# A fixed order on four engines, weights converted in small steps, and reciprocals on transposed sums

## The chip, the cores and the metric

The kernel runs on one core of a Trainium2 chip. TensorE (PE in the profile, with its weight loads as PEld) multiplies matrices, VectorE (DVE) and ScalarE (ACT) work element by element out of SBUF and PSUM, GpSimd (POOL) does so out of SBUF, and SyncE (SP) issues DMAs here. The engines run their own queues of instructions and wait for each other through semaphores. The metric is the device time of one execution in microseconds, the median of several; lower is better.

## The reference: what is computed

Attention over 4 batches and 8 heads with 768 positions and 64 dimensions, in which a query sees only the keys whose six hash bits are the same as its own; then a feed-forward layer over the 3072 rows of 512.

```python
q_bits = np.einsum('bhsd,dk->bhsk', q, proj) > 0        # 6 bits; k_bits likewise
mask = q_bucket[:, :, :, None] == k_bucket[:, :, None, :]
scores = np.where(mask, q @ k.T / np.sqrt(64), -1e9)
attn = np.exp(scores - scores.max(-1)); attn = attn / (attn.sum(-1) + 1e-9)
x = (attn @ v)                                          # as (3072, 512)
h = x @ w_in                                            # w_in (512, 2048), double precision
out = (h * (1 / (1 + np.exp(-1.702 * h)))) @ w_out      # w_out (2048, 512), double precision
```

q, k, v and proj come in single precision, the two weight matrices as 64-bit floats, which the kernel turns into 32-bit ones itself.

## The kernel before

**Pairs and units.** `attention` walks over 16 pairs: one batch and two heads, which lie on the two halves of the 128 partitions. A pair has two halves of 384 queries (`c` = 0, 1), and each half six blocks of 128 keys (`kt`). One (`c`, `kt`) is a unit; a pair has twelve. A unit is two bf16 matmuls on hash bits and two 32-bit ones on kT and qT into the score tile `ps` (L210, two buffers in PSUM), an exp on ACT from `ps` into the tile `e` (L211), a running sum `acc` of the exps on DVE (`sums`, L220 to L230, with POOL adding blocks 2 and 3 into `two`, L224), and the matmuls with v into `av` (L237). `values` runs two units behind `scores` (`LAG`). After the last unit of a half, `norm` sums `acc` over the partitions on PE (`dn`, L245), inverts all 128×384 sums (L247), and writes the quotient to `xT` (L249, L251).

**Preparing the next pair.** `steps_of(n + 1)` gives nine steps, one per unit of pair n: first `measure`, which on ACT squares k and q and keeps the largest sums (a guard read at the very end, L200); then for k and for q two groups of three PE transposes (`tp`, L155), copied to kT by DVE (L158) and to qT by ACT (L160), and two hash matmuls (L165), whose bits DVE writes (L166, L168). `tp`, `hash` and `dn` share two PSUM slots (tag `m`). k and q have one SBUF buffer each, so a load of the next k waits until both the transposes and `measure` are through with the last one. SP issues these loads.

**Weights.** `convert` turns a chunk of 128×512 doubles into floats: POOL issues its DMA (L104), DVE does six operations (L110 to L115 and L120), POOL a square (`size`, L118) and an addition (L119). There are 16 chunks of w_in and 16 of w_out. The text calls `convert` twice per pair.

**Order.** Only PE has its order written out (`manual_schedule(engines={PE})`); what stands on DVE, ACT, POOL and SP, and in which order, a scheduler decides by its own estimates.

**Feed-forward.** `feed_forward` takes six blocks of 512 rows: sixteen hidden tiles `h` (four matmuls each, L384, four PSUM buffers) with a gelu on ACT into `g` (L386), then four output tiles `y` (sixteen matmuls each, L390), copied by DVE (L393) and stored by SP. A second attention and a second feed-forward stand in an `If` that is taken only where `measure` found large values; it is not taken here.

Of the kernel before, what the change touches and what calls it, by code (L numbers as in the profile page):

```python
# [16 lines left out]
PE = mybir.EngineType.PE  # L17

P = 128
# [14 lines left out]
def kernel(  # L34
# [67 lines left out]
    def convert(cv, dst, src):  # L102
        raw = cv.tile([P, CW, 2], U32, tag="raw", name="raw", bufs=2)
        nc.gpsimd.dma_start(out=raw, in_=src)  # L104
        lo, hi = raw[:, :, 0], raw[:, :, 1]
        sign = cv.tile([P, CW], U32, tag="sign", name="sign")
        bits = cv.tile([P, CW], U32, tag="bits", name="bits")
        size = cv.tile([P, CW], F32, tag="size", name="size")

        nc.vector.tensor_scalar(sign, hi, 0x80000000, 0x40000000, op0=Alu.bitwise_and, op1=Alu.bitwise_or)  # L110
        nc.vector.tensor_scalar(bits, hi, 3, 0x7FFFFFFF, op0=Alu.logical_shift_left, op1=Alu.bitwise_and)  # L111
        nc.vector.tensor_tensor(bits, bits, sign, op=Alu.bitwise_xor)  # L112

        nc.vector.tensor_scalar(sign, bits, 0xFF800000, None, op0=Alu.bitwise_and)  # L114
        nc.vector.scalar_tensor_tensor(dst, lo, 2.0**-52, sign.bitcast(F32), op0=Alu.mult, op1=Alu.mult)  # L115


        nc.gpsimd.tensor_tensor(size, hi.bitcast(F32), hi.bitcast(F32), op=Alu.mult)  # L118
        nc.gpsimd.tensor_tensor(dst, bits.bitcast(F32), dst, op=Alu.add)  # L119
        nc.vector.scalar_tensor_tensor(dst, size, (1.125 * 2.0**-15) ** 2, dst, op0=Alu.is_ge, op1=Alu.mult)  # L120
# [3 lines left out]
    chunks = [(w_in_sb[:, kc, f : f + CW], wi[kc, :, f : f + CW]) for f in range(0, FF, CW) for kc in range(KC)]  # L124
    chunks += [(w_out_sb[:, fc, d : d + CW], wo[fc, :, d : d + CW]) for fc in range(FC) for d in range(0, DM, CW)]
# [13 lines left out]
    def prepare(wk, mps, tiles, scale, out_of):  # L139
# [5 lines left out]
        for name, off, op in (("k", k_off, Alu.is_gt), ("q", q_off, q_op)):  # L145
# [5 lines left out]
            def turned(c, name=name, x=x, xt=xt):  # L151
                cols = slice(c * HS, (c + 1) * HS)
                tp = mps.tile([P, HT, P], F32, tag="m", name="tp")
                for i in range(HT):
                    nc.tensor.transpose(tp[:, i, :], x[:, c * HT + i].rearrange("p j d -> p (j d)"), ident)  # L155
                tp = tp.rearrange("p t s -> p (t s)")
                if name == "k":
                    nc.vector.tensor_copy(xt[:, cols], tp)  # L158
                else:
                    nc.scalar.mul(xt[:, cols], tp, scale)  # L160
# [13 lines left out]
    def attention():  # L174
        actx = ExitStack()
        with actx:
            cv = actx.enter_context(tc.tile_pool(name="cv", bufs=1))
# [37 lines left out]
            def sums(n, c, kt):  # L215
                e = es[c]
                if kt == 1:
                    acc = st.tile([P, 2, HS], F32, tag="acc", name="acc")
                    accs[n, c] = acc
                    nc.vector.scalar_tensor_tensor(acc, e[:, 0, :, 0:HS], T * TINY, e[:, 1, :, 0:HS],  # L220
                                                   op0=Alu.add, op1=Alu.add)
                elif kt == 3:
                    two = st.tile([P, 2, HS], F32, tag="two", name="two", bufs=1)
                    nc.gpsimd.tensor_tensor(two, e[:, 2, :, 0:HS], e[:, 3, :, 0:HS], op=Alu.add)  # L224
                    accs[n, c, 2] = two
                elif kt > 3:
                    acc = accs[n, c]
                    nc.vector.tensor_tensor(acc, acc, e[:, kt, :, 0:HS], op=Alu.add)  # L228
                    if kt == T - 1:
                        nc.vector.tensor_tensor(acc, acc, accs.pop((n, c, 2)), op=Alu.add)  # L230
# [8 lines left out]

            def norm(n, c):  # L240
                b, hp = pairs[n]
                acc, av = accs.pop((n, c)), avs.pop((n, c))
                dn = mps.tile([P, HS], F32, tag="m", name="dn")
                for j in range(2):
                    nc.tensor.matmul(dn[D * j : D * (j + 1), :], ones, acc[:, j, :], start=True, stop=True)  # L245
                rd = st.tile([P, HS], F32, tag="rd", name="rd")
                nc.vector.reciprocal(rd, dn)  # L247
# [6 lines left out]
            def steps_of(n):  # L254
                ready[n] = {}
                return [lambda: measure(n)] + prepare(wk, mps, tiles[n], 1.0 / D**0.5, ready[n])

            with tc.manual_schedule(engines={PE}):
                fetch(0)
                for f in steps_of(0):  # L260
                    f()
                per = -(-len(chunks) // len(pairs))
                behind = []
                LAG = 2
                for n in range(len(pairs)):
                    todo = []
                    if n + 1 < len(pairs):
                        fetch(n + 1)
                        todo = steps_of(n + 1)
                    convs = chunks[n * per : (n + 1) * per]  # L270
                    for u in range(2 * T):
                        c, kt = divmod(u, T)
                        scores(n, c, kt)
                        behind.append((n, c, kt))
                        sums(n, c, kt)
                        if len(behind) > LAG:
                            x = behind.pop(0)
                            values(*x)
                            if x[2] == T - 1:
                                norm(x[0], x[1])  # L280
                        if u >= 1 and todo:
                            todo.pop(0)()
                        if u % 6 == 2 and convs:
                            convert(cv, *convs.pop(0))
                    for f in todo:
                        f()
                    for x in convs:
                        convert(cv, *x)
                for x in behind:
                    values(*x)  # L290
                    if x[2] == T - 1:
                        norm(x[0], x[1])

                nc.vector.tensor_reduce(largest, sizes, axis=AX.X, op=Alu.max)
                row = mps.tile([1, P], F32, tag="m", name="row")
                nc.tensor.transpose(row, largest, ident)
                nc.vector.tensor_reduce(largest[0:1, 0:1], row, axis=AX.X, op=Alu.max)
# [73 lines left out]
    def feed_forward(tag):  # L371
        NT = 512
        G = NT // P
        outv = out.rearrange("(b p t) d -> b t p d", b=B, p=P)
        with ExitStack() as fctx:
            gp = fctx.enter_context(tc.tile_pool(name=f"gp{tag}", bufs=2))
            op = fctx.enter_context(tc.tile_pool(name=f"op{tag}", bufs=4))
            fps = fctx.enter_context(tc.tile_pool(name=f"fps{tag}", bufs=4, space=PSUM))
            for n in range(N // NT):
                g = gp.tile([P, FC, NT], F32, tag="g", name="g")  # L380
                for fc in range(FC):
# [4 lines left out]
                    nc.scalar.activation(g[:, fc, :], h, Act.Gelu_apprx_sigmoid)  # L386
                for i in range(G):
# [9 lines left out]
    attention()  # L397
    feed_forward("")
# [32 lines left out]
```

## Time and profile before

| | us |
|---|---|
| median of 3 runs (1212.72 to 1213.97) | 1213.66 |
| the profiled execution | 1212.9 |
| its span, first to last instruction | 1211.1 |
| PE busy, share of the span | 1125.0, 93% |
| DVE busy | 437.9, 36% |
| ACT busy | 257.9, 21% |
| POOL busy | 160.6, 13% |
| mean granted clock of PE | 0.967 |

In the rows of the profile, `L247 DVE RECIPROCAL rd<-dn` names the line, the engine, the operation and the tile written and read; a group of equal instructions has its count, busy us, mean ns of one, and the idle time of the engine ahead of them with what ended it. Timeline rows begin with the start and the duration in us. A 32-bit matmul is two records, so that a hidden tile of four matmuls counts as eight. The busy shares are means over stages that differ, so the prediction reads them stage by stage.

### The profile page before, as it was taken

How to read it: one execution, taken by the hardware profiler on the slowest of the kernel's cores; microseconds unless marked ns; L12 is line 12 of the kernel's file. 1: busy time of each engine (PE TensorE's matmuls, PEld its weight loads, DVE VectorE, ACT ScalarE, POOL GpSimd, SP SyncE). 2: the span in 40 equal slices, each digit the busy share in tenths (PEclk: the TensorE clock that was granted, in tenths of full speed). 3: DMA queues.
4: the chain of work that ended last, by engine and by line, in shares of the span. 5: the costliest groups of instructions: out<-in, count | busy, mean ns of one | idle time of the engine just before them, and what ended most of it. 6: DMA issues, size and time to landing. Idle time of an engine off the chain costs nothing.

```text
span 1211.1 us, 9543 instructions
## 1 busy us (share of the span) xinstructions
PE 1125.0 (93%) x3905; PEld 456.5 (38%) x3905; DVE 437.9 (36%) x582; ACT 257.9 (21%) x386; POOL 160.6 (13%) x136
## 2 busy tenths in 40 slices
PE   5858677689999999989999999999999999999997
PEld 2222222233333333324444444444444444444443
DVE  6989899986666666660000000000000000000000
ACT  3322322234444444432100100110011001001100
POOL 4545454531111111110000000000000000000000
PEclk9788988889999999999999999999999999999999
DMA  7233223311212112000000000000000000000000
GB/s 171 75 94 109 80 94 96 96 44 40 53 42 50 40 40 53 14 2 0 1 17 18 0 9 17 9 1 9 27 0 1 17 18 0 9 17 9 1 18 19
DMA packets 83539, 42.64 MB, mean 35 GB/s; under 512 B 76320, under 2 KB 76320, under 8 KB 83488
## 3 DMA queue, kind: packets, MB, share of 16 engines
q1 hardware_dynamic: 78880, 25.18, 8.4%
q0 software_dynamic: 4608, 16.78, 3.9%
q8 instruction: 32, 0.52, 0.2%
q14 instruction: 19, 0.16, 0.0%
HBM read 35.65 MB, written 6.29 MB: 35 GB/s over the span
## 4 chain that ended last, share of the span: by engine, by line
PE 78%; DVE 18%; POOL 3%; issue 1%; DMA 1%; ACT 0%; DVEq 0%; POOLq 0%
PE h L384 27%; PE y L390 27%; PE ps L210 9%; PE av L237 8%; PE hash L165 3%; DVE bits L112 2%; DVE rd L247 2%; DVE acc L228 2%; DVE bits L111 2%; PE tp L155 1%; POOL w_in_sb L119 1%; PE dn L245 1%; POOL w_out_sb L119 1%; DVE sign L114 1%; DVE sign L110 1%
## 5 line engine op out<-in xcount | busy, mean ns | idle before, releaser
L384 PE MATMUL h<-xT,w_in_sb 128*128 128x512 f32 x768 | 332.3, 595 | 3.2 <-DVE xT L251 3.2
L390 PE MATMUL y<-w_out_sb,g 128*128 128x512 f32 x768 | 330.6, 592 | 0.0
L393 DVE COPY o<-y 128x512 f32<-128x512 f32 x24 | 16.6, 691 | 645.4 <-PE y L390 645.4
L384 PEld LDWEIGHTS h<-xT,w_in_sb 128*128 128x128 f32 x768 | 146.4, 191 | 187.7 <-issue 187.7
L390 PEld LDWEIGHTS y<-w_out_sb,g 128*128 128x128 f32 x768 | 145.9, 190 | 183.7 <-issue 183.7
L211 ACT ACTIVATE e<-ps 128x768 f32<-128x768 f32 x192 | 155.0, 809 | 206.7 <-PE ps L210 204.7
L386 ACT ACTIVATE g<-h 128x512 f32<-128x512 f32 x96 | 57.3, 597 | 542.7 <-PE h L384 542.7
L237 PE MATMUL av<-e,v 128*64 128x385 f32 x768 | 172.5, 530 | 0.0
L210 PE MATMUL ps<-qT,kT 64*128 64x384 f32 x768 | 163.7, 506 | 0.0
L228 DVE TENSOR_TENSOR acc<-acc,e 128x768 f32<-128x768 f32 x64 | 68.3, 1068 | 44.5 <-ACT e L211 44.4
L224 POOL TENSOR_TENSOR two<-e 128x768 f32<-128x768 f32 x32 | 50.6, 1581 | 252.7 <-ACT e L211 203.7
L245 PE MATMUL dn<-acc,ones 128*64 128x384 f32 x128 | 32.6, 594 | 53.7 <-DVE acc L230 53.7
L247 DVE RECIPROCAL rd<-dn 128x384 f32<-128x384 f32 x32 | 81.6, 2549 | 0.9 <-PE dn L245 0.9
L237 PEld LDWEIGHTS av<-e,v 128*64 128x64 f32 x768 | 39.1, 138 | 111.0 <-issue 110.8
L210 PEld LDWEIGHTS ps<-qT,kT 64*128 64x128 f32 x768 | 72.8, 199 | 0.2 <-issue 0.2
L210 PE MATMUL ps<-qb,kb 64*128 64x384 bf16 x384 | 66.5, 343 | 1.9 <-DVE qb L168 1.8
L210 PEld LDWEIGHTS <-kb 64*128 64x128 bf16 x384 | 18.7, 93 | 91.5 <-issue 84.1
L118 POOL TENSOR_TENSOR size<-raw 128x512 f32<-128x512 f32 x32 | 41.4, 1293 | 31.2 <-DVE w_out_sb L120 12.3
L165 PE MATMUL hash<-kT,pb 128*128 128x384 f32 x64 | 31.0, 572 | 5.9 <-DVE kT L158 5.9
L245 PEld LDWEIGHTS dn<-acc,ones 128*64 128x64 f32 x128 | 8.9, 154 | 69.5 <-DVE acc L230 62.5
L220 DVE SCALAR_TENSOR_TENSOR acc<-e 128x768 f32<-128x768 f32 x32 | 32.5, 1017 | 0.0
L230 DVE TENSOR_TENSOR acc<-acc,two 128x768 f32<-128x768 f32 x32 | 31.6, 988 | 1.3
(51 smaller groups left out, 463.8 us busy)
## 6 DMA issues: line engine op xcount, KB each, us to landing
raw<-in_moe_w_in_dram POOLq DMA_DIRECT2D x16, 512.0 KB, 3.8
raw<-in_moe_w_out_dram POOLq DMA_DIRECT2D x16, 512.0 KB, 3.5
k<-in_k_dram SPq DMA_DIRECT2D x32, 192.0 KB, 3.1
q<-in_q_dram SPq DMA_DIRECT2D x32, 192.0 KB, 3.3
v<-in_v_dram SPq DMA_DIRECT2D x32, 192.0 KB, 3.4
out_dram<-o SPq DMA_DIRECT2D x24, 256.0 KB, 2.0
pb<-in_proj_dram SPq DMA_DIRECT2D x2, 1.5 KB, 4.1
```

Of the source, the lines that this page charges most:

```text
L118: nc.gpsimd.tensor_tensor(size, hi.bitcast(F32), hi.bitcast(F32), op=Alu.mult)
L165: nc.tensor.matmul(dots, pb, xt[:, cols], start=True, stop=True)
L210: nc.tensor.matmul(ps[:, j, 0:HS], a[hs, keys], m[hs, cols], start=not last, stop=last)
L211: nc.scalar.activation(es[c][:, kt, :, 0:HS], ps[:, :, 0:HS], Act.Exp)
L224: nc.gpsimd.tensor_tensor(two, e[:, 2, :, 0:HS], e[:, 3, :, 0:HS], op=Alu.add)
L228: nc.vector.tensor_tensor(acc, acc, e[:, kt, :, 0:HS], op=Alu.add)
L237: nc.tensor.matmul(av[D * j : D * (j + 1), :], vt[:, kt, j, :], es[c][:, kt, j, :], start=(kt == 0), stop=(kt == T - 1))
L245: nc.tensor.matmul(dn[D * j : D * (j + 1), :], ones, acc[:, j, :], start=True, stop=True)
L247: nc.vector.reciprocal(rd, dn)
L384: nc.tensor.matmul(h, w_in_sb[:, kc, fc * P : (fc + 1) * P], xT[:, kc, n * NT : (n + 1) * NT], start=(kc == 0), stop=(kc == KC - 1))
L386: nc.scalar.activation(g[:, fc, :], h, Act.Gelu_apprx_sigmoid)
L390: nc.tensor.matmul(y, g[:, fc, i * P : (i + 1) * P], w_out_sb[:, fc, :], start=(fc == 0), stop=(fc == FC - 1))
```

## The change

- **Order.** PE, DVE, ACT and POOL all follow the order of the program's text, in attention and in the first feed-forward. Only SP's is still scheduled. The loop is written unit by unit: `scores` of unit u, `sums` of u−1, `values` of u−2 with `total` (the sum over partitions), `invert` of u−3 and `norm` of u−4.
- **Preparation.** `measure` is the last of the nine steps, not the first. ACT copies kT too.
- **Sums.** POOL's `two` is gone; DVE adds every block to `acc`.
- **Reciprocal.** All 32 sums of one column block are alike on 32 partitions after the matmul with ones. `invert` transposes `dn` in 32×32 blocks, inverts one column per block (128×12), and transposes the repeated result back to 128×384.
- **Weights.** `convert` is a generator with one operation or two per step; a pair converts one chunk of w_in, its steps spread over units 4 to 9. SP issues its DMA, ACT computes the square. The 16 chunks of w_out are converted in the feed-forward, one behind each of the first sixteen gelus, and `convert`'s tiles stay allocated through it.
- **Feed-forward.** `hidden(n + 1)` stands ahead of `outputs(n)`; `o` has three buffers, not four.

```diff
-    def convert(cv, dst, src):
+    def convert(dst, src):
         raw = cv.tile([P, CW, 2], U32, tag="raw", name="raw", bufs=2)
-        nc.gpsimd.dma_start(out=raw, in_=src)
+        nc.sync.dma_start(out=raw, in_=src)
...
+        nc.scalar.activation(size, hi.bitcast(F32), Act.Square)
+        yield
         nc.vector.scalar_tensor_tensor(dst, lo, 2.0**-52, sign.bitcast(F32), op0=Alu.mult, op1=Alu.mult)
-        nc.gpsimd.tensor_tensor(size, hi.bitcast(F32), hi.bitcast(F32), op=Alu.mult)
+        yield
         nc.gpsimd.tensor_tensor(dst, bits.bitcast(F32), dst, op=Alu.add)
...
-                if name == "k":
-                    nc.vector.tensor_copy(xt[:, cols], tp)
-                else:
-                    nc.scalar.mul(xt[:, cols], tp, scale)
+                nc.scalar.mul(xt[:, cols], tp, 1.0 if name == "k" else scale)
...
+            def invert(n, c):
+                dn = accs.pop((n, c))
+                rt = st.tile([P, HS], F32, tag="rt", name="rt", bufs=1)
+                nc.vector.transpose(rt, dn)
+                r = st.tile([P, HS // 32, 1], F32, tag="r", name="r")
+                nc.vector.reciprocal(r, rt.rearrange("p (s i) -> p s i", i=32)[:, :, 0:1])
+                rd = accs[n, c] = st.tile([P, HS], F32, tag="rd", name="rd", bufs=1)
+                nc.vector.transpose(rd.rearrange("p (s i) -> p s i", i=32), r.to_broadcast([P, HS // 32, 32]))
...
+            for u in range(len(units) + 4):
+                if u < len(units):
+                    n, c, kt = units[u]
+                    if (c, kt) == (0, 0):
+                        whole(conv)
+                        if n + 1 < len(pairs):
+                            fetch(n + 1)
+                            todo = steps_of(n + 1)
+                        conv = convert(*in_chunks[n])
+                        next(conv)
+                    scores(n, c, kt)
+                if 1 <= u <= len(units):
+                    sums(*units[u - 1])
+                if 2 <= u <= len(units) + 1:
+                    values(*units[u - 2])
+                    if units[u - 2][2] == T - 1:
+                        total(*units[u - 2][:2])
+                if 3 <= u <= len(units) + 2 and units[u - 3][2] == T - 1:
+                    invert(*units[u - 3][:2])
+                if 4 <= u and units[u - 4][2] == T - 1:
+                    norm(*units[u - 4][:2])
+                if u < len(units):
+                    if (c, kt) != (0, 0) and todo:
+                        todo.pop(0)()
+                    if 2 * c * T + kt >= 4:
+                        next(conv, None)
...
                     nc.scalar.activation(g[:, fc, :], h, Act.Gelu_apprx_sigmoid)
+                    if convs:
+                        for _ in convert(*convs.pop(0)):
+                            pass
...
+            hidden(0)
+            for n in range(N // NT):
+                if n + 1 < N // NT:
+                    hidden(n + 1)
+                outputs(n)
+
+    with tc.manual_schedule(engines=ORDERED):
+        attention()
+        feed_forward("", out_chunks)
```

What stands in a row now shows at three places. DVE before, in the second half of pair 1 (`e_111` is that half's exps; the lines L110 to L120 are `convert`):

```order
L110 TENSOR_SCALAR sign<-raw 128x512
L120 SCALAR_TENSOR_TENSOR w_in_sb<-size,w_in_sb 128x512
L111 TENSOR_SCALAR bits<-raw 128x512
L228 TENSOR_TENSOR acc<-acc,e_111 128x768
L112 TENSOR_TENSOR bits<-bits,sign 128x512
L114 TENSOR_SCALAR sign<-bits 128x512
L115 SCALAR_TENSOR_TENSOR w_in_sb<-raw,sign 128x512
L228 TENSOR_TENSOR acc<-acc,e_111 128x768
L120 SCALAR_TENSOR_TENSOR w_in_sb<-size,w_in_sb 128x512
L230 TENSOR_TENSOR acc<-acc,two 128x768
L110 TENSOR_SCALAR sign<-raw 128x512
L111 TENSOR_SCALAR bits<-raw 128x512
```

And DVE now, from unit 4 to unit 8 of a pair (L115 to L125 are `convert`, L229 and L225 the sums of the exps `e_112` and `e_113`, L250 to L254 `invert`):

```order
L115 TENSOR_SCALAR sign<-raw 128x512
L116 TENSOR_SCALAR bits<-raw 128x512
L229 TENSOR_TENSOR acc<-acc,e_112 128x768
L118 TENSOR_TENSOR bits<-bits,sign 128x512
L229 TENSOR_TENSOR acc<-acc,e_112 128x768
L121 TENSOR_SCALAR sign<-bits 128x512
L173 TENSOR_SCALAR qb<-hash,q_off 128x384
L175 TENSOR_SCALAR qb<-qb 128x384
L125 SCALAR_TENSOR_TENSOR w_in_sb<-raw,sign 128x512
L225 SCALAR_TENSOR_TENSOR acc<-e_113 128x768
L250 STREAM_TRANSPOSE rt<-dn 128x384
L252 RECIPROCAL r<-rt 128x12
```

Where two chunks and the start of a third stood within two units, one chunk now lies between the sums of a pair. On ACT, the place of `measure` (`junk`) in a pair before:

```order
L160 ACTIVATE qT<-tp 128x384
L211 ACTIVATE e_111<-ps 128x2x384
L200 ACTIVATE junk,sizes<-q 128x768
L211 ACTIVATE e_111<-ps 128x2x384 x3
L211 ACTIVATE e_110<-ps 128x2x384 x5
L200 ACTIVATE junk,sizes<-k 128x768
```

and now, with the copies of kT and the square of `convert` (`size`) in the same queue:

```order
L167 ACTIVATE qT<-tp 128x384
L217 ACTIVATE e_113<-ps 128x2x384
L167 ACTIVATE qT<-tp 128x384
L123 ACTIVATE size<-raw 128x512
L217 ACTIVATE e_113<-ps 128x2x384 x3
L206 ACTIVATE junk,sizes<-k 128x768
L206 ACTIVATE junk,sizes<-q 128x768
L217 ACTIVATE e_113<-ps 128x2x384 x2
```

Both squares of `measure` moved together behind the fourth exp of the second half, after the last transpose of q. On ACT in the feed-forward, where before 96 gelus stood in one row behind one table load, there now stands:

```order
L217 ACTIVATE e_113<-ps 128x2x384 x5
L401 ACT_TABLE_LOAD
L401 ACTIVATE g<-h 128x512
L123 ACTIVATE size<-raw 128x512
L401 ACTIVATE g<-h 128x512
L123 ACTIVATE size<-raw 128x512
```

Sixteen such couples follow each other, then the other gelus; each square moved in between two gelus.

More of the change, by code (lines that the diff above doesn't have):

```diff
@@ L16 @@
 PSUM = bass.MemoryType.PSUM
-PE = mybir.EngineType.PE
+E = mybir.EngineType
+ORDERED = {E.PE, E.DVE, E.Activation, E.Pool}
 P = 128
@@ L255, in steps_of @@
                 ready[n] = {}
[L256 to L297, printed above, removed]
```

61 lines of the change are left out of this document (37 added, 24 removed).

## The prediction

> **What bounds the kernel now.** I first read busy time by stage (columns: stretch, its length, busy us of PE, PEld, DVE, ACT and POOL with instruction counts, granted TensorE clock, DMA share, GB/s).
>
> ```profile
> 60.00:120.00 60.00, 41.50 (x194) 13.96 (x190) 54.75 (x74) 15.10 (x22) 29.17 (x25) 0.83 0.34 101
> 180.00:262.00 82.00, 60.56 (x289) 20.64 (x290) 75.69 (x103) 23.83 (x35) 40.63 (x34) 0.85 0.27 82
> 320.00:380.00 60.00, 60.00 (x328) 21.46 (x326) 40.92 (x50) 27.82 (x41) 7.79 (x5) 1.00 0.19 43
> 543.90:1211.10 667.20, 661.13 (x1536) 292.32 (x1536) 16.59 (x24) 58.60 (x97) 0.00 (x0) 1.00 0.03 10
> ```
>
> There are three stages. Up to 262 us DVE is busy 54.75 of 60 us and PE waits; from 262 to 544 PE is busy all the time; from 544 the feed-forward is PE alone. The chain of waits and the timeline of DVE give the length of one pair in the first two (start, duration, what):
>
> ```profile
> 136.66 2.47 DVE rd L247
> 179.66 2.47 DVE rd L247
> ...
> 275.18 0.16 DVE L249 COPY vs<-av 128x1 f32<-128x1 f32 x1 [1.35 <-PE av L237]
> 302.28 0.16 DVE L249 COPY vs<-av 128x1 f32<-128x1 f32 x1 [1.35 <-PE av L237]
> ```
>
> Each half of a pair has one reciprocal and one such copy, so two reciprocals further is one pair: 43.0 us while DVE sets the pace, 27.1 us while PE does. What makes DVE slow is in its first rows:
>
> ```profile
> 5.65 0.43 DVE L110 TENSOR_SCALAR sign<-raw 128x512 uint32<-128x512 uint32 x1 [3.78 <-DMA raw<-in_moe_w_in_dram]
> 5.99 1.26 DVE L111 TENSOR_SCALAR bits<-raw 128x512 uint32<-128x512 uint32 x1
> 7.29 0.69 DVE L112 TENSOR_TENSOR bits<-bits,sign 128x512 uint32<-128x512 uint32 x1
> 8.02 0.43 DVE L114 TENSOR_SCALAR sign<-bits 128x512 uint32<-128x512 uint32 x1
> 8.48 0.69 DVE L115 SCALAR_TENSOR_TENSOR w_in_sb<-raw,sign 128x512 f32<-128x512 uint32 x1
> 10.54 0.69 DVE L120 SCALAR_TENSOR_TENSOR w_in_sb<-size,w_in_sb 128x512 f32<-128x512 f32 x1 [1.38 <-POOL w_in_sb L119]
> ...
> 5.70 1.27 POOL L118 TENSOR_TENSOR size<-raw 128x512 f32<-128x512 f32 x1 [3.24 <-DMA raw<-in_moe_w_in_dram]
> 9.25 1.26 POOL L119 TENSOR_TENSOR w_in_sb<-bits,w_in_sb 128x512 f32<-128x512 f32 x1 [2.28 <-DVE w_in_sb L115]
> ```
>
> One chunk of weights costs DVE 0.43 + 1.26 + 0.69 + 0.43 + 0.69 + 0.69 = 4.19 us, and all 32 are converted by 262 us, five or more to a pair.
>
> **The change, part by part.** *Attention: what DVE keeps.* Costs of the removed and added work:
>
> ```profile
> L247 DVE RECIPROCAL rd<-dn 128x384 f32<-128x384 f32 x32 | 81.6, 2549 | 0.9 <-PE dn L245 0.9
> L230 DVE TENSOR_TENSOR acc<-acc,two 128x768 f32<-128x768 f32 x32 | 31.6, 988 | 1.3
> L158 DVE COPY kT<-tp 128x384 f32<-128x384 f32 x32 | 16.9, 532 | 5.3 <-PE tp L155 5.3
> L160 ACT ACTIVATE qT<-tp 128x384 f32<-128x384 f32 x32 | 15.7, 491 | 60.9 <-PE tp L155 60.9
> L386 ACT ACTIVATE g<-h 128x512 f32<-128x512 f32 x96 | 57.3, 597 | 542.7 <-PE h L384 542.7
> L200 ACT ACTIVATE junk<-k 128x768 bf16<-128x768 f32 x16 | 13.5, 843 | 31.5 <-DMA k<-in_k_dram 31.5
> ```
>
> A pair without conversion costs DVE 40.92/60 of 27.1 = 18.5 us. Out go two reciprocals (5.1) and two copies of kT (1.06). In comes one accumulation more per half, since POOL's sum of two blocks is gone: 2 × 0.99 = 2.0. One chunk per pair adds 4.2. The inversion is now a 32×32 transpose of 128×384 out of PSUM, a reciprocal of 128×12 and a transpose back. The reciprocal costs about 0.2 us (12/384 of 2.55 is 0.08, and the 128×1 copy takes 0.16). No row shows a transpose on DVE: from below the nearest is L158, 0.53 us for the same shape out of PSUM; from above L247, 2.55. I take 0.55, since it moves each element once, as the copy does. [...] So DVE comes to 18.5 − 5.1 − 1.06 + 2.0 + 4.2 + 4 × 0.55 + 0.4 = 21.1 us per pair, or 29.1 at 2.55. ACT has 27.82/60 of 27.1 = 12.6, plus two copies of kT (0.98) and one square of 128×512 (0.60 like L386, at most L200's 0.84): 14.2 us. POOL keeps one addition. PE's work is the same, 27.1 us. **PE is therefore the bound of every pair**, not of ten in sixteen, and 27.1 is what I use.
>
> Where this is hidden work, the cover is PE's 27.1 us against 21.1, six us per pair; without it, each us costs 16.
>
> *Does the fixed order make PE wait?* Units of PE (scores, then the values of two units before) and the wide sum:
>
> ```profile
> 404.64 0.87 PE L237 MATMUL av<-e,v 128*64 128x385 f32 x4
> 405.44 0.34 PE L210 MATMUL ps<-qb,kb 64*128 64x384 bf16 x2
> 406.36 0.87 PE L237 MATMUL av<-e,v 128*64 128x385 f32 x4
> ...
> 410.47 0.81 PE L245 MATMUL dn<-acc,ones 128*64 128x384 f32 x4
> 411.22 0.34 PE L210 MATMUL ps<-qb,kb 64*128 64x384 bf16 x2
> ```
>
> A unit is 1.72 us (0.80 of it values), a sum 0.75. The tight places are three. (1) The two squares of `measure` now stand on ACT behind the exp of the tenth unit, about 1.9 us, with the next two exps queued behind them. PE asks for that score buffer 4.2 us after the tenth scores; exp 0.8 + 1.9 + exp 0.8 leaves 0.7 us. (2) The second three transposes of k stand one unit after `dn` and need the slot that ACT's copy of the first three frees: about 0.9 us to spare. (3) The loads of k for pair n+2 wait for `measure`:
>
> ```profile
> 280.22 1.23 SPq L135 DMA_DIRECT2D k<-in_k_dram  x2
> ...
> DMA to landing us min/median/max: 2.7/3.2/5.7
> ```
>
> Exp 0.8, square and its read 1.0, two issues 1.23, landing 3.2: k is there 6.2 us after the tenth scores, and PE transposes it after four more units and a sum, at 8.4. Only the longest landing (5.7) would overrun, by 0.3 us. The weight chunk's DMA in the same SP queue is issued two units ahead of k and waits for nothing later. I cost all three at nothing; from above 2 us per pair, 30 in all.
>
> *Start and end of attention.*
>
> ```profile
> 11.76 2.93 PE L165 MATMUL hash<-kT,pb 128*128 128x384 f32 x4 [3.68 <-DVE kT L158]
> ...
> 19.38 0.34 PE L210 MATMUL ps<-qb,kb 64*128 64x384 bf16 x2 [1.83 <-DVE qb L168]
> ...
> 515.57 0.34 PE L210 MATMUL ps<-qb,kb 64*128 64x384 bf16 x2
> ...
> 538.62 0.96 DVE L230 TENSOR_TENSOR acc<-acc,two 128x768 f32<-128x768 f32 x1
> ...
> 540.54 2.56 DVE L247 RECIPROCAL rd<-dn 128x384 f32<-128x384 f32 x1 [0.90 <-PE dn L245]
> ...
> 543.90 16.53 PE L384 MATMUL h<-xT,w_in_sb 128*128 128x512 f32 x34 [3.21 <-DVE xT L251]
> ```
>
> With no chunk on DVE ahead of kT (L120 ran until 11.23) and ACT copying it, most of 3.68 goes, 3.4, and about 0.5 of the 1.83 where L112 stood ahead of qb: first scores at 15.5. Pair 1's k now waits for `measure` too, which I put at 1.0. The last pair takes 543.90 − 515.57 = 28.3 today. L230 and its gap go (1.06), the inversion shrinks from 2.56 to 1.3, and the reduction of `sizes`, its transposition on PE and the second reduction now stand ahead of h (0.8, estimated): 26.8. Pair 0 lacks a sum and two units' values (2.4). So h starts at 15.5 + 1.0 + 15 × 27.1 − 2.4 + 26.8 = **447.4** instead of 543.9.
>
> *Feed-forward: sixteen chunks of w_out behind the first sixteen gelus.*
>
> ```profile
> 543.90 56.87 PE h L384 x128
> 600.77 54.93 PE y L390 x128
> ...
> 549.42 1.28 ACT L386 ACT_TABLE_LOAD   x1 [11.89 <-PE h L384]
> 550.71 0.60 ACT L386 ACTIVATE g<-h 128x512 f32<-128x512 f32 x1
> ```
>
> PE makes an h in 54.93/16 = 3.43 us (the first sixteen 1.94 slower). On ACT gelu f, square f, gelu f+1 follow each other; square f needs the size buffer, freed by L120 of chunk f−1. So gelus go at DVE's pace per chunk, while PE may run four h buffers ahead. That pace is the quoted chunk, 5.65 to 11.23 = 5.58, less 0.84 by which L111 was longer than L110 while POOL ran L118, now gone, less 0.08 by which the next chunk's first operation starts before L120 ends: 4.65 us. Chunk 0 ends 8.8 us after h starts (gelu 0 ends at 551.31, 7.4 in; square 0.6; L120 0.7). The gelu that frees PE's 21st h ends at 8.8 + 14 × 4.65 + 1.4 = 75.3; PE would have come at 1.94 + 20 × 3.43 = 70.5. **PE loses 4.8 us**, in gaps of some 1.2, then nothing more: w_out is whole at about 79, and the first y now stands behind two blocks of h, at 117. At 5.58 per chunk the loss is 17.8. The chunk's DMA, now on SP, may take 6.5 us before it sets the pace; the rows have 5.7 at most. That hidden(n+1) stands ahead of outputs(n), and three `o` buffers in place of four, cost nothing: one y takes 13.7 us of PE.
>
> [...]
>
> **Sum.** The span was 1211.1 and the profiled execution 1212.9, 1.8 more. New span: 447.4 + 667.2 + 4.8 = 1119.4; execution 1121.2. The median of the runs shown, 1213.66, lies 0.8 above the profiled one: **1122**.
>
> **Rivals.** *PE waits in each pair* (the 0.7, 0.9 and 2.2 us of slack do not hold, or transposes near 2.55 make DVE 29.1 us): 1 to 2 us × 15 to 16, 1137 to 1153. For it: three engines in strict order, each blocking what stands behind. Against: PE's order is already fixed and never waited between 320 and 380. *The feed-forward goes at 5.58 per chunk*: 1135. *The clock stays low*: PE at 0.83 as in the row 60 to 120 makes a pair 32.7 us, 15 × 5.6 = 83 more, 1205. Against: wherever PE was busy throughout it is 1.00. [...] *Slower than before*: DVE's transposes are so slow that DVE sets the pace. To lose 92 us each pair must take 32.9, that is (32.9 − 18.9)/4 = 3.5 us per transpose, above even the reciprocal; from there on it is slower than 1214. *The change does not do what it says* (chunks still crowd DVE): about 1213; the fixed order excludes it nearly.
>
> **How the numbers follow.** Forecast (1112 to 1135) 0.68; waits in each pair 0.17; slow chunks 0.06; clock 0.05; no effect 0.01; slow transposes 0.03. The range 1112 to 1155 takes in the first three and the upper bounds of the transposes, the chunk and the waits; below 1112 PE's own work would have to shrink. Of this kernel a measurement tells about 0.2% from no change: faster 0.96, same 0.01, slower 0.03.
>
> **What would show it.** PE busy nearly 27.1 us of every pair from about 20 us on at a clock of 1.00, h starting near 447, STREAM_TRANSPOSE near 0.55 us, POOL's addition in the feed-forward near 1.26, the gelus 4.65 apart from about the fifth to the sixteenth, four short waits of PE for ACT near 507 to 522. Wrong would be: PE idle behind k's DMA or an exp in each pair, DVE above 27 us per pair, or chunks above 5 us.

## The result, and the profile after

The changed kernel takes **1121.65 us** (1120.01 to 1122.54, median of four runs) where the kernel before takes 1213.82 (1212.72 to 1214.48) beside it on the same chip: a ratio of **0.924, 95% interval 0.9224 to 0.9256**. The prediction was 1122. The profiled execution took 1122.28 with a span of 1120.4, 90.7 us shorter than before.

Busy time by stage of the kernel after (columns as in the prediction's first table):

```profile
60.00:120.00 60.00, 60.00 (x328) 21.53 (x326) 41.61 (x73) 29.29 (x45) 5.75 (x3) 1.00 0.26 66
180.00:262.00 82.00, 82.00 (x450) 29.75 (x450) 56.09 (x96) 41.92 (x64) 5.75 (x3) 1.00 0.26 63
448.22:1120.40 672.18, 662.05 (x1536) 291.98 (x1536) 67.43 (x120) 67.67 (x113) 20.26 (x16) 1.00 0.06 21
```

PE, at 41.50 of 60 us and 60.56 of 82 in the first two stretches before, is now busy all the time at full clock. Its own work has become shorter too: for the same 3905 matmul records it was busy 1125.0 us before and is busy 1099.1 now. So of the 90.7 us, 64.8 are time in which PE stood idle, and 25.9 are work that went slower between the waits, at a granted clock of 0.83 to 0.89 in the stretches before 262 us.

The length of a pair is read from DVE's timeline, two copies of `vs` apart (the row for the other half of the pair lies between):

```profile
93.87 0.15 DVE L260 COPY vs<-av 128x1 f32<-128x1 f32 x1
...
120.97 0.15 DVE L260 COPY vs<-av 128x1 f32<-128x1 f32 x1
```

That is 27.10 us, in the stage in which a pair took 43.0. All that PE waited for in the whole execution stands in the view of waits (who waited for whom, us in all, times, the longest):

```profile
PE tp L165 <- DMA k<-in_k_dram: 8.0, 2, 5.7
PE h L399 <- ACT g L401: 3.8, 4, 1.0
PE row L308 <- DVE largest L306: 2.4, 1, 2.4
PE h L399 <- DVE largest L309: 0.4, 1, 0.4
PE ps L216 <- DVE qb L175: 0.3, 1, 0.3
```

No wait that repeats by pair is left: the first load of k (5.7), pair 1's k (2.4), the end of attention (2.4 and 0.4) and four waits in the feed-forward. PE's timeline gives the borders of the stages: first transposes, first scores, the transposes of pair 1's k, the last pair's first scores, and h:

```profile
5.67 1.52 PE L165 MATMUL tp<-ident,k 128*128 128x128 f32 x6 [5.67 <-DMA k<-in_k_dram]
...
13.19 0.34 PE L216 MATMUL ps<-qb,kb 64*128 64x384 bf16 x2 [0.32 <-DVE qb L175]
...
17.35 0.53 PE L165 MATMUL tp<-ident,k 128*128 128x128 f32 x3 [2.37 <-DMA k<-in_k_dram]
...
421.36 0.34 PE L216 MATMUL ps<-qb,kb 64*128 64x384 bf16 x2
...
448.22 60.15 PE L399 MATMUL h<-xT,w_in_sb 128*128 128x512 f32 x136 [0.37 <-DVE largest L309]
```

| stage, us | predicted | measured |
|---|---|---|
| to the first scores | 15.5 | 13.19 |
| fifteen pairs, with the wait for pair 1's k | 1.0 + 15 × 27.1 − 2.4 = 405.1 | 421.36 − 13.19 = 408.2 |
| last pair, to h | 26.8 | 448.22 − 421.36 = 26.9 |
| feed-forward | 667.2 + 4.8 = 672.0 | 672.2 |
| span | 1119.4 | 1120.4 |

Against before, attention ends 95.7 us earlier (543.90 to 448.22) and the feed-forward is 5.0 longer (667.2 to 672.2).

### The profile page after: what moved, and what is told of

It is laid out like the page before. It is cut to its first block, busy times and chain, and to the rows that moved or that the text cites. A ratio compares the mean times of both kernels' runs of the same rounds, so it can differ in the third digit from the quotient of the medians.

```text
span 1120.4 us, 9656 instructions
## 1 busy us (share of the span) xinstructions
PE 1099.1 (98%) x3905; PEld 451.1 (40%) x3905; DVE 368.3 (33%) x646; ACT 290.0 (26%) x450; POOL 51.1 (5%) x40
## 4 chain that ended last, share of the span: by engine, by line
PE 92%; DVE 4%; POOL 2%; issue 1%; DMA 1%; ACT 0%; SPq 0%; ACTq 0%; DVEq 0%
PE y L411 29%; PE h L399 24%; PE ps L216 16%; PE av L236 14%; PE hash L172 5%; PE tp L165 3%; PE dn L243 2%; POOL w_out_sb L127 2%; DVE bits L118 1%; DVE w_out_sb L125 1%; DMA k<-in_k_dram 1%; DVE sign L121 1%; DVE sign L115 1%; DVE bits L116 0%; ACT L401 0%
## 5 line engine op out<-in xcount | busy, mean ns | idle before, releaser
L236 PE MATMUL av<-e,v 128*64 128x385 f32 x768 | 166.9, 514 | 0.0
L216 PE MATMUL ps<-qT,kT 64*128 64x384 f32 x768 | 155.8, 484 | 0.0
L229 DVE TENSOR_TENSOR acc<-acc,e 128x768 f32<-128x768 f32 x128 | 122.2, 954 | 15.6 <-ACT e L217 12.3
L216 PEld LDWEIGHTS ps<-qT,kT 64*128 64x128 f32 x768 | 69.8, 191 | 0.2 <-issue 0.2
L216 PEld LDWEIGHTS <-kb 64*128 64x128 bf16 x384 | 18.5, 92 | 85.7 <-issue 85.6
L127 POOL TENSOR_TENSOR w_in_sb<-bits,w_in_sb 128x512 f32<-128x512 f32 x16 | 30.0, 1875 | 404.5 <-DVE w_in_sb L125 404.5
L225 DVE SCALAR_TENSOR_TENSOR acc<-e 128x768 f32<-128x768 f32 x32 | 30.6, 955 | 24.5 <-ACT e L217 24.5
L173 DVE TENSOR_SCALAR qb<-hash,q_off 128x384 bf16<-128x384 f32 x32 | 19.1, 598 | 55.7 <-PE hash L172 55.7
L173 DVE TENSOR_SCALAR kb<-hash,k_off 128x384 bf16<-128x384 f32 x32 | 19.8, 618 | 44.5 <-PE hash L172 44.5
L123 ACT ACTIVATE size<-raw 128x512 f32<-128x512 f32 x32 | 21.5, 672 | 43.8 <-DVE w_out_sb L130 43.8
L172 PE MATMUL hash<-qT,pb 128*128 128x384 f32 x64 | 29.0, 537 | 0.0
L243 PE MATMUL dn<-acc,ones 128*64 128x384 f32 x128 | 26.1, 487 | 0.0
```

Source lines behind the costliest of these rows:

```text
L172: nc.tensor.matmul(dots, pb, xt[:, cols], start=True, stop=True)
L173: nc.vector.tensor_scalar(bits[:, cols], dots, 0.0, off[:, 0:1], op0=op, op1=Alu.subtract)
L216: nc.tensor.matmul(ps[:, j, 0:HS], a[hs, keys], m[hs, cols], start=not last, stop=last)
L236: nc.tensor.matmul(av[D * j : D * (j + 1), :], vt[:, kt, j, :], es[c][:, kt, j, :], start=(kt == 0), stop=(kt == T - 1))
```

## The experiments

The theory: **chunks crowded into the first pairs cost the time, and PE's own 27.1 us set a pair once nothing stands late in front of it.** The rivals: it is the reciprocals and the other work taken from DVE; it is the fixed order as such; what is left over is bound by something else. Each kernel was timed beside the kernel before (1211 to 1216 us in all of these runs). Diffs are against the changed kernel where not said otherwise.

**The old reciprocal.**

```diff
-                nc.vector.transpose(rt, dn)
...
-                nc.vector.reciprocal(r, rt.rearrange("p (s i) -> p s i", i=32)[:, :, 0:1])
...
-                nc.vector.transpose(rd.rearrange("p (s i) -> p s i", i=32), r.to_broadcast([P, HS // 32, 32]))
+                nc.vector.reciprocal(rd, dn)
```

> The changed kernel with the old inversion: one reciprocal of 128x384 out of dn in place of transpose, reciprocal of 128x12, transpose. Theory (PE sets every pair and DVE has some six us to spare): DVE gets 2 x (2.55 - 1.39) = 2.3 us more per pair, 23 to 24 in all, the period stays 27.1, and only the last pair shows it, by 1.2 us: 1122.8. Rival (the reciprocals were what held the kernel up): 16 x 2.3 = 37 us more, 1158.

It took 1122.89, ratio 0.9258 (0.9243 to 0.9274). Its windows:

```profile
60.00:120.00 60.00, 60.00 (x330) 21.48 (x328) 47.32 (x64) 31.10 (x49) 5.74 (x3) 1.00 0.26 67
```

DVE is busy 47.32 us in place of 41.61, and PE still all 60. Only the wait at the end of attention grows, from 2.35 to 3.42. By that wait the new reciprocal is worth one microsecond here, not 37; the interval of the ratio overlaps that of the changed kernel.

**Five chunks per pair, in the fixed order.**

```diff
+            def several(chunks):
+                for x in chunks:
+                    yield from convert(*x)
+                    yield
+            PER = 5
...
-                        conv = convert(*in_chunks[n])
-                        next(conv)
+                        conv = several((in_chunks + out_chunks)[PER * n : PER * (n + 1)])
+                        next(conv, None)
...
-                    if 2 * c * T + kt >= 4:
-                        next(conv, None)
+                    if c * T + kt >= 1:
+                        for _ in range(4):
+                            next(conv, None)
...
-        feed_forward("", out_chunks)
+        feed_forward("")
```

> The changed kernel, with all 32 chunks converted in attention, five to a pair from the first pair on, four steps per unit, in the fixed order; none in the feed-forward. Theory (chunks crowded into the first pairs are what cost the time before): DVE needs 16.9 + 5 x 4.2 = 37.9 us in six pairs, 10.8 more than PE, 65 us in all, less the 4.9 us of the feed-forward: 1182, and up to 1225 if DVE also waits for POOL's addition in each chunk. Rival (the fixed order is what matters, where the chunks stand does not): 1117 to 1125.

**Only PE's order fixed.** (in attention; the feed-forward is scheduled whole, as in the kernel before)

```diff
-    with tc.manual_schedule(engines=ORDERED):
+    with tc.manual_schedule(engines={E.PE}):
         attention()
-        feed_forward("", out_chunks)
+    feed_forward("", out_chunks)
```

> The changed kernel with only PE's order fixed: DVE, ACT and POOL go back to the scheduler, which puts all 32 chunks into the first eleven half-pairs, as it did before the change; every other part of the change stays. Theory (crowding costs the time): DVE needs 16.9 + 5.8 x 4.2 = 41 us in five and a half pairs, 14 more than PE, 78 us, less 4.9 of the feed-forward: 1195, between 1180 and 1210. Rival (the work taken from DVE and POOL, reciprocals first, is the gain): 1122 to 1140.

They took 1178.9 (ratio 0.972) and 1181.76 (0.9741). The windows from 60 to 120 us, first of the five chunks per pair, then of the free order:

```profile
60.00:120.00 60.00, 51.62 (x238) 17.29 (x236) 47.33 (x87) 25.67 (x41) 12.72 (x8) 0.86 0.31 90
```

```profile
60.00:120.00 60.00, 47.56 (x226) 16.17 (x224) 54.55 (x93) 25.14 (x43) 13.31 (x9) 0.90 0.42 115
```

Both have the lighter DVE, the new reciprocal and kT on ACT, and they lose 57 and 60 us of the 92. One has the fixed order, the other not: with the chunks crowded in both they differ by 3 us. So the fixed order is worth what the places written into it are worth. The way of the loss is not the same. The largest waits of PE, first of the five chunks per pair, then of the free order:

```profile
PE dn L243 <- DVE acc L229: 38.1, 12, 4.3
```

```profile
PE tp L165 <- ACT kT L167: 20.1, 5, 4.8
```

In the fixed order the sums come late. In the free order ACT's copies of kT do: they stand behind squares that wait for DVE's last operation on the chunk before (the square at 138.57 us waits 3.45, the copy follows at 139.15, and PE has waited 4.77). DVE is not full in either, at 47.33 and 54.55 of 60 us, so counting its work, as my theory did, does not give the whole mechanism, and that 1182 was so near 1178.9 is partly luck. PE's own work is 20.9 and 15.2 us longer than in the changed kernel (1120.0 and 1114.3 us busy), at a granted clock of 0.86 and 0.90 in these windows.

**The kernel before, with its order fixed.** (against the kernel before)

```diff
-            with tc.manual_schedule(engines={PE}):
+            with tc.manual_schedule(engines={PE, mybir.EngineType.DVE, mybir.EngineType.Activation, mybir.EngineType.Pool}):
```

> The kernel before, with nothing but the order of DVE, ACT and POOL fixed to its text in attention: two whole chunks per pair, old reciprocals, two sums on POOL, POOL's square. Theory (spread chunks are the gain): DVE needs 18.5 + 2 x 4.2 to 5.0 = 26.9 to 28.5 us per pair, and waits for POOL's addition in each chunk up to 1.4 us: 27 to 31.5 per pair, so attention takes 435 to 505 us in place of 524: 1125 to 1195. Rival (without the small steps and the lighter DVE the fixed order brings nothing): 1205 to 1225.

It took 1194.37, ratio 0.985 (0.9832 to 0.9869), the upper end of the theory's range. The placing, two whole chunks per pair, gains 18 us, and then the order of the text gets in the way. PE's waits, and one stretch of POOL and DVE:

```profile
PE dn L245 <- DVE acc L230: 33.7, 17, 4.2
PE hash L165 <- DVE kT L158: 23.0, 15, 2.3
```

```profile
307.70 1.54 POOL L224 TENSOR_TENSOR two<-e 128x768 f32<-128x768 f32 x1
307.77 2.01 DVE L120 SCALAR_TENSOR_TENSOR w_out_sb<-size,w_out_sb 128x512 f32<-128x512 f32 x1 [1.37 <-POOL w_out_sb L119]
```

L120 waits 1.37 us for POOL's addition, and then takes 2.01 in place of 0.69 beside POOL's `two`, which began 0.07 earlier; kT's copy and `acc` stand behind it. All 32 of these L120 average 2.01 us.

| | before's operations and steps | the change's |
|---|---|---|
| DVE, ACT and POOL scheduled | 1212.88 | 1181.76 |
| order of the text | 1194.37 | 1121.65 |

(The last value is from the changed kernel's own runs, the others from one series.) The order alone gives 18.5, the rest alone 31, both 91: neither is the cause by itself. The order of the text is not the same in the two columns: it is that of each kernel.

**Two chunks per pair, no chunk in the feed-forward.** As the five per pair, with two steps per unit from the fifth unit on:

```diff
+            PER = 2
...
+                    if c * T + kt >= 4:
+                        for _ in range(2):
+                            next(conv, None)
```

> The changed kernel with all 32 chunks converted in attention, two to a pair, two steps per unit, and none in the feed-forward. Theory (PE sets a pair as long as DVE has less than its 27.1 us): DVE has 41.6/60 of 27.1 = 18.8, plus 4.2 = 23.0 us; the period stays 27.1 and the four waits of the feed-forward (4.9 us) go: 1116.8. Rival (in the strict order PE waits as soon as DVE waits for POOL's addition, 1.9 us twice in a pair): 1 to 4 us per pair more, 1133 to 1180.

1147.29, ratio 0.9449 (0.9434 to 0.9464): the rival's result. Its windows and PE's waits:

```profile
60.00:120.00 60.00, 56.97 (x311) 20.24 (x308) 44.77 (x78) 29.89 (x46) 9.10 (x5) 1.00 0.31 83
```

```profile
PE dn L243 <- DVE acc L229: 25.0, 16, 2.3
```

DVE has a quarter of its time left, and still PE waits once in each pair, and a pair takes 28.83 us (`vs` at 98.39 and 127.22) in place of 27.10. The timeline shows the place:

```profile
301.70 1.92 POOL L127 TENSOR_TENSOR w_out_sb<-bits,w_out_sb 128x512 f32<-128x512 f32 x1 [9.58 <-DVE w_out_sb L125]
...
303.65 0.69 DVE L130 SCALAR_TENSOR_TENSOR w_out_sb<-size,w_out_sb 128x512 f32<-128x512 f32 x1 [1.16 <-POOL w_out_sb L127]
...
306.33 0.87 PE L243 MATMUL dn<-acc,ones 128*64 128x384 f32 x4 [1.50 <-DVE acc L229]
```

L130 waits for POOL in front of the last additions to `acc`; they come late, and `dn` on PE, with everything behind it, later still.

**One step of a chunk per unit.** Still two chunks per pair, but each step has a unit of its own, and each load is issued a chunk ahead:

```diff
         lo, hi = raw[:, :, 0], raw[:, :, 1]
+        yield
...
-        yield
...
+            def stream(chunks):
+                gens = [convert(*x) for x in chunks]
+                next(gens[0])
+                yield
+                for i, gen in enumerate(gens):
+                    if i + 1 < len(gens):
+                        next(gens[i + 1])
+                    for _ in gen:
+                        yield
+                    yield
...
+            todo, conv = [], stream(in_chunks + out_chunks)
+            next(conv)
...
-                    if 2 * c * T + kt >= 4:
-                        next(conv, None)
+                    next(conv, None)
```

> The changed kernel with all 32 chunks converted in attention, two to a pair as in e3_two_per_pair, but one step of a chunk per unit through all twelve units, each chunk's load issued a chunk ahead; none in the feed-forward. e3_two_per_pair took 1147 where 1117 was expected: PE waited 25 us for `acc`, while DVE was busy only 44.8 of 60 us. Theory (what counts is what stands ahead of `acc`'s last addition in DVE's queue: L130 waits 1.16 us for POOL there, not DVE's load): with two units between L125 and L130 PE does not wait, the period is 27.1 and the feed-forward has no waits: 1116 to 1118. Rival (23 us of DVE per pair are too many for a strict order): 1135 or more.

1126.74, ratio 0.9285 (0.9269 to 0.9301), between the two. With the same operations per pair, the wait for `acc` falls from 25.0 to 5.9 us in all, so place and not load made most of the 25. But 0.33 us of waiting per pair stay, and a pair takes 27.65 (`vs` at 67.37 and 95.02), 0.55 more than in the changed kernel; sixteen times that is 8.8 of the 9 to 11 us above the theory's 1116 to 1118. The timeline shows what of the addition on POOL still reaches `acc`:

```profile
317.61 2.90 DVE L229 TENSOR_TENSOR acc<-acc,e 128x768 f32<-128x768 f32 x2
317.77 1.92 POOL L127 TENSOR_TENSOR w_out_sb<-bits,w_out_sb 128x512 f32<-128x512 f32 x1 [14.07 <-DVE w_out_sb L125]
```

Two additions to `acc` that take 0.95 each elsewhere take 2.90 here; the second ends at 320.51, 0.82 after POOL. That this delay makes the 0.33 us of wait is read from the order of the rows; it was not tried apart.

**The square back on POOL.**

```diff
-        nc.scalar.activation(size, hi.bitcast(F32), Act.Square)
+        nc.gpsimd.tensor_tensor(size, hi.bitcast(F32), hi.bitcast(F32), op=Alu.mult)
```

> The changed kernel with the square of `size` back on POOL, nothing else. Theory of the feed-forward's loss (the gelus wait behind the squares on ACT, which wait for DVE's last operation of the chunk before): without a square on ACT no gelu waits for a chunk, PE never waits, although a chunk takes longer, up to 5.6 us; w_out is whole at 95 after the start of h, before the first y at 117; in attention DVE's extra 0.84 lies under PE: 1116.8. Rival (a chunk's length is what sets the loss, as the 5.58 us case of the prediction has it): 1135. Second rival (POOL's square blocks DVE and so PE in each pair, 0.8 us or more): 1130 or more.

**Two buffers for `size`.**

```diff
-        size = cv.tile([P, CW], F32, tag="size", name="size")
+        size = cv.tile([P, CW], F32, tag="size", name="size", bufs=2)
```

> The changed kernel with two buffers of `size` in place of one. Theory: the square of chunk f waits for DVE's end of chunk f-2, so the gelus may run one chunk (4.66 us) further ahead; the four waits of PE were 4.9 us in all, so at most 0.3 remain: 1117.0. Rival (the gelus wait for something else, the raw loads or `bits`): 1121.6 as before.

Beside both, the changed kernel was timed again.

> The changed kernel as it is, timed beside the three below on the same chip: 1120 to 1123, with a span of 1120.4 in the profile.

It took 1120.59, ratio 0.9241 (0.9225 to 0.9258), with a span of 1116.7 in its profile; where the 3.7 us to the first profile lie is in the last section. The square on POOL took 1115.07 (0.9189, 0.9176 to 0.9202), two buffers 1119.39 (0.9223, 0.921 to 0.9237), which the time alone does not tell from the changed kernel. With the square on POOL a chunk is slower, and in the feed-forward PE does not wait for it at all; DVE's and PE's timelines:

```profile
453.71 1.27 DVE L116 TENSOR_SCALAR bits<-raw 128x512 uint32<-128x512 uint32 x1
```

```profile
448.85 111.34 PE L399 MATMUL h<-xT,w_in_sb 128*128 128x512 f32 x255 [0.37 <-DVE largest L309]
```

L116 takes 1.27 us beside POOL's square, and chunks are 5.5 us apart (L115 at 453.37 and 458.88), but the hidden tiles run through in one piece (the view ends at 560 us). From h to the end it is 1116.2 − 448.85 = 667.4 us in place of 672.2. With two buffers one wait of 1.0 us is left of the four, and the feed-forward takes 1117.5 − 448.69 = 668.8; I had expected a rest of at most 0.3.

**Two buffers for k, and the square on POOL.**

```diff
-            x = ld.tile([P, T, 2, D], F32, tag=name, name=name, bufs=v_bufs if name == "v" else 1)
+            x = ld.tile([P, T, 2, D], F32, tag=name, name=name, bufs=1 if name == "q" else v_bufs)
```

> The changed kernel with two buffers for k, so that the next pair's k is loaded without waiting for `measure`, and with the square on POOL as in e4_square_pool. Theory: at the start PE neither waits some 2 us for the second k nor runs at half clock after that (1.9 us), so pair 0 takes 24.7 in place of up to 28.7, and h starts at 443 to 445; with the 4.9 us of the feed-forward: 1112 to 1114. Rival (the start is bound by the loads themselves, which share the queue): 1115 to 1117, as with the square on POOL alone.

**1111.17 us, ratio 0.9169** (0.9152 to 0.9186), the fastest of all and a little under the theory's 1112 to 1114, though its interval still touches that of the square on POOL alone; what the second buffer does is read from the trace. PE's timeline has no wait between the first scores and the end of attention:

```profile
12.94 0.34 PE L216 MATMUL ps<-qb,kb 64*128 64x384 bf16 x2 [0.29 <-DVE qb L175]
...
444.01 110.13 PE L399 MATMUL h<-xT,w_in_sb 128*128 128x512 f32 x256 [0.37 <-DVE largest L309]
```

**POOL's sum, and DVE's copy of kT, each put back alone.**

```diff
+                elif kt == 3:
+                    two = st.tile([P, 2, HS], F32, tag="two", name="two", bufs=1)
+                    nc.gpsimd.tensor_tensor(two, e[:, 2, :, 0:HS], e[:, 3, :, 0:HS], op=Alu.add)
...
+                    if kt == T - 1:
+                        nc.vector.tensor_tensor(acc, acc, accs.pop((n, c, 2)), op=Alu.add)
```

> The changed kernel with POOL's sum `two` of blocks 2 and 3 back, so that DVE has one accumulation less per half, and adds `two` last. Theory (a pair is PE's 27.1 us whatever POOL does): 1120 to 1123. Rival (DVE's operations with two inputs wait while POOL adds, as in e9_before_ordered, where DVE's L120 took 2.01 us beside `two` in place of 0.69, and the last addition to `acc` then comes too late for PE): 0.5 to 1.5 us per half, 1137 to 1170.

```diff
-                nc.scalar.mul(xt[:, cols], tp, 1.0 if name == "k" else scale)
+                if name == "k":
+                    nc.vector.tensor_copy(xt[:, cols], tp)
+                else:
+                    nc.scalar.mul(xt[:, cols], tp, scale)
```

> The changed kernel with DVE copying kT out of PSUM, as before the change. Theory (0.53 us twice a pair lie under PE's cover): 27.1 per pair, at most 1 us at the start: 1120 to 1123. Rival (in a strict order the copy stands behind DVE's other work and PE's hash waits for it, as in e9_before_ordered, where that was 23 us): 0.5 to 1.5 us per pair, 1129 to 1146.

1124.24 (0.9269, 0.9252 to 0.9286) and 1122.06 (0.9252, 0.9233 to 0.9271): neither can be told from the changed kernel for certain. The one new wait with the sum on POOL comes once, at the very end:

```profile
PE dn L249 <- DVE acc L235: 0.9, 1, 0.9
```

Yet POOL's sum does meet the last operation on the chunk here too: in attention L130, the L120 of the kernel before, takes 1.32 us on average with the sum on POOL and 0.68 without (at 91.90 us 1.34, beside a `two` that began at 91.15). It costs nothing, since DVE's next addition to `acc`, at 93.53, still waits 0.29 us for its exp; in the kernel before with its order fixed, kT's copy and `acc` stood right behind it. kT's copy, in turn, has no whole chunk in front of it. What was costly there was the neighbourhood, not the operation. Four parts were not tried apart: the raw loads' move from POOL's to SP's queue, the new place of `measure`, `hidden(n + 1)` ahead of `outputs(n)`, and three `o` buffers in place of four.

## Why the prediction was right, step by step

**PE is the bound of every pair, at 27.1 us: right**, and it carries the result. 27.10 us measured; chunks crowded five or six to a pair bring most of the loss back (1178.9, 1181.76), the old reciprocal does not (1122.89).

**DVE's 21.1 us per pair: too high, without effect.** 41.61/60 of 27.1 is 18.8. The new operations were sized well, the chunk not:

```profile
L254 DVE STREAM_TRANSPOSE rd<-r 128x384 f32<-128x384 f32 x32 | 18.5, 578 | 1.1
L250 DVE STREAM_TRANSPOSE rt<-dn 128x384 f32<-128x384 f32 x32 | 18.4, 576 | 1.0 <-PE dn L243 1.0
L116 DVE TENSOR_SCALAR bits<-raw 128x512 uint32<-128x512 uint32 x32 | 13.5, 421 | 0.0
L252 DVE RECIPROCAL r<-rt 128x12 f32<-128x12 f32 x32 | 7.3, 229 | 1.1
```

A transpose takes 0.58 (0.55 taken, bounds 0.53 to 2.55), the small reciprocal 0.23 (0.2 taken). I had 1.26 for L116 in a pair, which is its time beside POOL's square; alone it takes 0.42, 0.84 less. Another 0.9 lay in the 18.5 I started from: the second operation on `qb` (L168) took 0.71 on average between 320 and 401 us, 1.60 and 1.63 in the two cases where it began 0.05 and 0.03 us behind POOL's `two` and 0.26 in the others, and takes 0.26 now that `two` is gone, twice per pair. The remaining half us was not traced.

**"The cover is PE's 27.1 us against 21.1, six us per pair": the weak sentence.** Load alone does not tell what is covered. In the 60 us from 60 on, the old reciprocals raise DVE from 41.61 to 47.32, which is 21.4 us per pair, and cost nothing; one more chunk per pair brings it to nearly the same, 21.5 (44.77 of 60, at 28.83 per pair), and costs 1.7 us per pair, because its last step waits for POOL ahead of `acc`. The change's own order avoids this, but the rival of "1 to 2 us per pair" was nearer than I took it to be, and needed no slow transposes.

**The three tight places: right.** In the waits of PE there is no exp, no copy by ACT, and one load of k only, at the start.

**The start: wrong twice, in opposite directions.** First scores came 2.3 us earlier than forecast: k landed 0.9 earlier (PE's first transposes began at 5.67, before at 6.56, two executions' loads), the hash waited for nothing at all (3.7 gone, 3.4 taken), and the wait for qb shrank by 1.5, not 0.5. Pair 0 then lost 3.1 more: the wait for pair 1's k was 2.37 where I put 1.0, and behind it PE ran at half clock, which the sum had no term for:

```profile
18.10:19.60 1.50, 1.50 (x8) 0.42 (x8) 0.00 (x0) 0.30 (x1) 0.00 (x0) 0.50 0.00 0
```

That the span still came out within 1.0 us is partly luck: these two errors nearly cancel, and the half clock comes in some executions and not in others.

**End of attention and feed-forward: right.** 26.9 for the last pair (26.8 forecast). PE's loss comes in four gaps; three of its restarts, and gelus and squares on ACT:

```profile
513.97 3.70 PE L399 MATMUL h<-xT,w_in_sb 128*128 128x512 f32 x8 [0.95 <-ACT g L401]
518.63 3.70 PE L399 MATMUL h<-xT,w_in_sb 128*128 128x512 f32 x8 [0.96 <-ACT g L401]
523.30 41.47 PE L399 MATMUL h<-xT,w_in_sb 128*128 128x512 f32 x96 [0.96 <-ACT g L401]
```

```profile
475.48 0.69 ACT L123 ACTIVATE size<-raw 128x512 f32<-128x512 f32 x1 [3.49 <-DVE w_out_sb L130]
476.08 0.58 ACT L401 ACTIVATE g<-h 128x512 f32<-128x512 f32 x1
480.14 0.69 ACT L123 ACTIVATE size<-raw 128x512 f32<-128x512 f32 x1 [3.48 <-DVE w_out_sb L130]
```

A gelu stands behind a square that waits 3.5 us for DVE; the cadence is 4.66 (4.65 forecast). That the 0.84 by which L111 was longer would go was an estimate of mine; L116 takes 0.41 to 0.43 here, with nothing of POOL's beside it. PE's h are 4.66 apart in place of 3.43: 1.23 each, 4.9 in all (4.8 forecast), of which the waits show 3.8; the rest is that a tile by itself is recorded with 3.70 us, against 3.43 in a row. The square on POOL shows that this coupling, not the length of a chunk, is the cause: chunks of 5.5 us cost nothing there. The rival of 5.58 us per chunk with the square on ACT was not tried.

**Two slips that changed nothing.** The upper end of "1 to 2 us × 15 to 16" is 1154, not 1153. And PE was busy throughout from 262 to 320 us before, too, where the granted clock was 0.98, not 1.00.

## What to carry to other kernels

Find the engine whose work sets the period, and spread the others' side work until each has less than that; then look at what stands directly ahead of the operation that this engine waits for, since a wait of 1.2 us for a third engine cost 1.7 us of every pair there, while 2.3 us of plain work elsewhere cost nothing. A fixed order is worth what its places are worth: it brought 18 us with the old places and 60 with the new places and operations. And where a side task shares a queue with a consumer (the square ahead of the gelu), moving it to a slower but uncoupled engine can be the faster choice: here chunks 5.5 us apart in place of 4.66, and 1115.07 us in place of 1120.59.

## What the runs showed of the hardware

**Short gaps and the clock.** In pair 0 the half clock came after gaps of PE of 1.96 us (two chunks per pair, and one step per unit), 2.29 (two buffers for `size`), 2.37 (the changed kernel) and 2.44 (the square on POOL), and not in every execution. The same gap of 2.37 us as in the changed kernel cost nothing with the old reciprocal; PE's timeline and the windows of that kernel:

```profile
17.06 0.52 PE L165 MATMUL tp<-ident,k 128*128 128x128 f32 x3 [2.37 <-DMA k<-in_k_dram]
```

```profile
18.00:21.00 3.00, 3.00 (x21) 1.07 (x17) 0.96 (x1) 1.68 (x4) 0.00 (x0) 1.00 0.00 0
```

Full clock also stood behind 1.71, 2.19 (the sum on POOL) and 2.64 us (kT on DVE). The gap of 1.71 is that of the changed kernel's second profile, which kept full clock at the start of h too: h began at 446.26 and its first seventeen tiles took 58.65, against 448.22 and 60.15 in the first, which makes 3.5 of the 3.7 us between the spans. Where the clock fell in pair 0, it was 0.50 for 3.4 us in four of the five profiles (17.8 to 21.2 in the changed kernel); with the square on POOL it fell at 18.7 and was still 0.50 at 21.9. Ahead of h, PE has a gap of 2.35 us and, after one matmul, one of 0.37 in both profiles of the changed kernel: in the first the clock was 0.50 from 447.8 to 451.3, in the second it stayed at 1.00. With the old reciprocal, where the longer of the two is 3.42, it was 0.50 from 446.0 to 452.9. The four gaps of 0.95 in the feed-forward never showed it (1.00 from 508.3 to 524 us), nor did the gaps of some 1.5 us, one in each pair, with two chunks per pair (1.00 from 60 to 120 and from 320 to 380 us). So the length of a gap alone does not tell here whether the clock falls; what else decides it no run settles.

**POOL and DVE beside each other.** An operation of one that begins while the other is in one was often the longer for it:

```profile
L127 POOL TENSOR_TENSOR w_in_sb<-bits,w_in_sb 128x512 f32<-128x512 f32 x16 | 30.0, 1875 | 404.5 <-DVE w_in_sb L125 404.5
L127 POOL TENSOR_TENSOR w_out_sb<-bits,w_out_sb 128x512 f32<-128x512 f32 x16 | 20.3, 1266 | 69.9 <-DVE w_out_sb L125 69.9
```

The same addition on POOL takes 1.88 us on average in attention, where in fifteen of sixteen cases it begins 0.16 or 0.17 behind one of DVE's sums (L225 at 415.21 and POOL at 415.37, in one pair) and takes 1.91 or 1.92; in the sixteenth and in the feed-forward, with nothing of DVE's beside it, it takes 1.26 or 1.27. The other way round DVE paid: 2.01 for 0.69 beside `two`, 1.27 for 0.42 beside a square on POOL. Before the change L111 took 1.26 at 255.00, behind an L118 begun at 254.82, and 1.25 at 143.95, behind a `two` begun at 143.34; where it began first, at 59.73 with L118 at 59.90, it took 0.42. Of its 32, sixteen began while POOL was in no square or addition, and took 0.41 or 0.42; of the other sixteen, thirteen took 0.73 to 1.30 and three 0.42 or 0.43, one of these at 184.11, behind an L118 begun at 183.95. So beginning second does not always cost, and why those three did not pay no run here settles.
